# Wider step ranges for the projection blocks of a fused double attention, and its first output made in two passes

## The chip, the core and the metric

The kernel runs on one core of a Trainium2 chip. The core has a matrix engine (TensorE, PE in the profile; its weight loads are PEld), a vector engine (VectorE, DVE), a scalar engine (ScalarE, ACT), a general engine (GpSimd, POOL) and a sequencer that here issues nearly all DMAs (SyncE, SP). The metric is the device time of one execution in microseconds (us), lower is better.

## The reference

Two attentions, A and B, each with 32 heads of 20 features, read the same x; a gate mixes their results.

```python
x = A_x                                          # 1 x 2048 x 640
g = sigmoid((x * gate_w).sum(-1, keepdims=True))
def mha(x, wqkv, wo):                            # A_wqkv, A_wo or B_wqkv, B_wo
    qkv = (x @ wqkv).reshape(1, 2048, 3, 32, 20)
    q, k, v = ...                                # each 1 x 32 x 2048 x 20
    p = softmax(q @ k^T * 20 ** -0.5)
    return (p @ v).reshape(1, 2048, 640) @ wo
return g * mha(x, A_wqkv, A_wo) + (1 - g) * mha(x, B_wqkv, B_wo)
```

Inputs and output are float32.

## The kernel before

**Tiling.** The 64 heads of both attentions are taken in 16 groups of four (index g; groups 0 to 7 are A's, z = 0, groups 8 to 15 are B's, z = 1). The queries of a group are taken in four blocks of 512 (qb), and the 2048 keys in eight pairs of tiles of 128. One pair of key tiles, for one query block and four heads, is a **step** G; there are 16 x 4 x 8 = 512 steps, 32 to a group. Below, b is the first step of a group.

**What a step does.** Eight score matmuls (line 632) go into PSUM banks, and ACT turns each into weights with an exponential (`pt`, line 635). The step also applies the weights of the step before to the values: sixteen matmuls into `acc` (line 650), in two groups, V. And, some 15 steps ahead, it computes the row maxima that the softmax subtracts: eight matmuls (line 574), whose results DVE reduces (`mpart`, line 585); some go through ACT and a custom DVE operation first (lines 578, 582). When the maxima of a query block are complete, `finish_max` writes them to DRAM (`m_scr`, line 606) and back as four extra rows of the queries' tile QT (line 610), so that the score matmul itself subtracts them; the scores of that query block cannot begin before these rows are there.

**Blocks.** The projections have to be made beside the attention. They are cut into blocks of matmuls (line 375), one PSUM bank each: `project_a` makes keys and the first 48 query features of a group (4 chunks of 512 rows, three blocks of 15 matmuls each, drained by ACT into `fs`, line 402, and split by POOL into two float16 parts, `cq`); `project_r` makes the remaining query features of four groups (`rk`); `project_v` makes the values of two groups (two blocks to a pair of row tiles). `out_tiles` makes a row tile of an output: its blocks multiply stored attention results (`o_in`) with `wo`. The sum over features is cut into jobs; a job that is not the first loads the partial result `y_scr`, adds to it on DVE (line 717) and stores it again; the first one scales on ACT (line 715).

**What sets the order.** Everything is placed at build time. `fill` holds entries (first step, due step, number of blocks, generator). `slot` takes the able entry that is due first and puts out one block. Each step's order is one of three strings in `STEP`: without a block, with one (X at the start) and with two (X at both ends). Which one is decided by `behind`: two if, taking able entries by due step, their blocks do not fit one a step. `at` and `tasks` place other work (weight loads, weight maxima, splits) at given steps.

**Spreading.** Once two chunks of `project_a` are there, `later` copies them by DMA from `cq` and `rk` into the rows of QT and KT (`spread`, lines 421 and 423, all issued by SP), two halves of 18 copies each, and four copies of key differences into KD. It starts no earlier than step b+1 of the group before the one it is for, because QT and KT have two buffers and the group before that one has just finished with its own.

Of the kernel before, what the change touches and what calls it, by code (L numbers as in the profile page):

```python
# [21 lines left out]
D = 640  # L22
H = 32
DH = 20
NT = S // P
NC = D // P
GH = 4
NG = H // GH
GF = GH * DH
QB = 512  # L30
NQ = S // QB
# [3 lines left out]
VW = DH + 1  # L35
XE = 7
QKS = 2.0 ** -12
PARTS = (0, 176, 344, 512)
OB = 3
OWAIT = 20  # L40
SUM0, SUM1 = -8, 1.9


STEP = ("e0 m1 V e1 m0 e0 m1 e1 m0 e0 m1 e1 m0 V e0 m1 e1 m0",
# [17 lines left out]
def kernel(  # L62
# [148 lines left out]
    def scales_qk(i, maxima):  # L211

        return scales(maxima, 2, lambda r, inv: set_qk(i, r, inv))
# [114 lines left out]
    def weights_a(g):  # L328

        st = {}  # L330

        def load():
            i = g % NG
            t = st["t"] = wts.tile([P, NC, 160], F32, name="wstage", tag="wstage", bufs=2)
            w = wqkv[g // NG].rearrange("(c p) f -> p c f", p=P)
            nc.sync.dma_start(t[:, :, 0:GF], w[:, :, D + i * GF:D + (i + 1) * GF])
            nc.sync.dma_start(t[:, :, GF:P], w[:, :, i * GF:i * GF + 48])

        def split():
            hi, lo = blk["a", g] = block_tiles("a")  # L340
            for c0, c1, part in ((0, GF, 1), (GF, P, 0)):
                split_weights(st["t"][:, :, c0:c1], r_qk[g // 4][:, part:part + 1], hi[:, :, c0:c1], lo[:, :, c0:c1],
                              2 - 2 * part)

        return load, split
# [4 lines left out]
    def weights_r(i):  # L350

        st = {}

        def load():
            t = st["t"] = wts.tile([P, NC, 160], F32, name="wstage", tag="wstage", bufs=2)
            w = wqkv[i // 2].rearrange("(c p) f -> p c f", p=P)
            for j in range(4):
                f = (4 * (i % 2) + j) * GF + 48
                nc.sync.dma_start(t[:, :, 32 * j:32 * j + 32], w[:, :, f:f + 32])

        def split():
            hi, lo = blk["r", i] = block_tiles("r")
            rest_tiles(i)
            split_weights(st["t"][:, :, :P], r_qk[i][:, 0:1], hi, lo)

        return load, split

    def mms(i, out_ap, pairs, cost):

        if now[0] >= 0:  # L370
            tick_block(len(pairs) * cost * T_SCORE, free_at[i])
        for k, (a, b) in enumerate(pairs):
            if now[0] < 0:
                tick_block(cost * T_SCORE, free_at[i])
            nc.tensor.matmul(out_ap, a, b, start=(k == 0), stop=(k == len(pairs) - 1))  # L375
            if now[0] < 0:
                yield
# [3 lines left out]
        for _ in range(n if now[0] >= 0 else 0):  # L381
            yield

    def project_chunk(w, hi, lo, ch):

        wh, wl = w
        def pairs(n):
            if now[0] < 0:
                return ([(wh[:, c, :], b[:, c, n]) for c in range(NC) for b in (xh, xl)]
                        + [(wl[:, c, :], xh[:, c, n]) for c in range(NC)])  # L390
            return [(a[:, c, :], b[:, c, n]) for c in range(NC) for a, b in ((wh, xh), (wh, xl), (wl, xh))]

        t0 = ch * QB
        if now[0] >= 0:
            f = work.tile([P, QB], F32, name="fs")
            for k in range(3):
                if k:
                    yield
                m = slice(PARTS[k], PARTS[k + 1])
                i, pt = take()  # L400
                yield from mms(i, pt[:, m], pairs(slice(t0 + m.start, t0 + m.stop)), 0.34)
                nc.scalar.activation(f[:, m], pt[:, m], AF.Copy, scale=QKS)  # L402
                give(i, spend("act", 0.25, clock["done"]))
            nc.gpsimd.tensor_copy(hi, f)  # L404
            nc.gpsimd.tensor_tensor(lo, f, hi, op=OP.subtract)
        else:
            i, pt = take()
            yield from mms(i, pt, pairs(slice(t0, t0 + QB)), 1)
            give(i, spend("dve", T_MAX, spend("act", T_EXP, clock["done"])))
            nc.scalar.activation(hi, pt, AF.Copy, scale=QKS)  # L410
            nc.vector.scalar_tensor_tensor(lo, pt, QKS, hi, op0=OP.mult, op1=OP.subtract)
# [33 lines left out]

    def project_r(i, ch):
        n = slice(ch * QB, (ch + 1) * QB)
        yield from project_chunk(blk["r", i], rk[i][:, 0, n], rk[i][:, 1, n], ch)
        r_done.add((i, ch))

    def half_tiles(g):
# [22 lines left out]
    def project_a(g, ch):  # L474
        if ch % 2 == 0:
            half_tiles(g)
        hl = blk["q", g]
        n = slice((ch % 2) * QB, (ch % 2 + 1) * QB)
        yield from project_chunk(blk["a", g], hl[:, 0, n], hl[:, 1, n], ch)
        if ch == 1:  # L480
            key_differences(g, hl, work.tile([P, QB], F32, name="fs"), work.tile([P, 2, QB], F16, name="dd", bufs=1))
        if ch % 2 == 1:
            def later():
                for _ in range(10):
                    yield
                while not {(g // 4, c) for c in (ch - 1, ch)} <= r_done or now[0] < (g - 1) * NQ * NS + 1:
                    yield
                if ch == 1:
                    yield from spread_differences(g)
                yield from spread(g, hl, ch // 2 * 1024, 1024)  # L490
                spread_done.add((g, ch // 2))

            side.append(later())
# [478 lines left out]
    def at(G, f):  # L972
        todo.setdefault(G, []).append(f)
# [5 lines left out]
    def tasks(G, gap, fs):  # L979
        for k, f in enumerate(fs):  # L980
            at(G + k * gap, f)

    at(4, sigmoids)
    for g in range(2 * NG):
        b = g * NQ * NS
        n = g + 1
        if n < 2 * NG:
            fill += [(b - 8, b + 4 + ch, 3, project_a(n, ch)) for ch in range(4)]
            if n + 1 < 2 * NG:
                tasks(b + 15, 3, weights_a(n + 1))  # L990
            i = g // 4 + 1
            if i < 4:
                if g % 4 == 0:
                    z, c0 = i // 2, 320 * (i % 2)
                    parts = max_tasks([[(wqkv[z], part * D + c0 + 160 * k) for k in range(2)] for part in range(2)],
                                      lambda m, i=i: scales_qk(i, m))
                    tasks(b + 2, 2, parts)
                if g % 4 == 2:
                    tasks(b + 18, 3, weights_r(i))
                if g % 4 == 3:  # L1000
                    fill += [(b - 9, b + 4 + ch, 3, project_r(i, ch)) for ch in range(4)]
            gg = g // 2 + 1
            if gg < NG and g % 2 == 0:
                load, scale, split = weights_v(gg)
                at(b, load)
                at(b + 3, lambda scale=scale: side.append(scale()))
                at(b + 7, split)
                fill += [(b + 10, b + 14 + 3 * j, 2, project_v(gg, j)) for j in range(0, NT, 2)]
    for z in range(2):
        b = (6, 12)[z] * NQ * NS  # L1010
        parts = max_tasks([[(wo[z], 160 * k) for k in range(4)]], lambda m, z=z: scales_o(z, m), wrow[z])
        tasks(b + 8, 1, parts)
        b = ((NG - 1) * NQ * NS + 4, (NG + 5) * NQ * NS - 4)[z]
        for i in range(4):
            tasks(b + 3 * i, 2, out_weights(z, i))
    at((2 * NG - 1) * NQ * NS + 9, last_weights)
    at(STEPS - 4, last_picks)


    jobs = [(0, 0, NC, True, y_scr), (1, 0, 3, False, y_scr), (1, 3, NC, False, y_sum)]  # L1020
    step = NQ * NS
    outs = [(NG * step + 2 + int(9 * t), jobs[0], t) for t in range(NT)]
    outs += [((NG + 5) * step + 8 + int(3.3 * t), jobs[1], t) for t in range(NT)]
    outs += [((NG + 7) * step + SUM0 + int(SUM1 * t), jobs[2], t) for t in range(NT)]
    flow = []

    def features_stored(job, t):
# [4 lines left out]
    def out_tasks(G):  # L1032
        flow[:] = [f for f in flow if "done" not in f]
        over = (2 * NG - 1, 1) in spread_done and {(NG - 1, j) for j in range(NT)} <= v_done
        if outs and outs[0][0] <= G and len(flow) < (OB if outs[0][1][4] is y_sum else 2) and features_stored(*outs[0][1:]) and (
                over or outs[0][1][4] is not y_sum):
            G0, job, t = outs.pop(0)
            state = {"due": G0 + 10}
            flow.append(state)
            side.append(out_tiles(job, t, state))  # L1040
        if last and all(4 * last[0][0] + t in summed for t in range(4)):
            soon(now[0] + 6, 4, last_tiles(*last.pop(0)))
# [134 lines left out]
```

## Time and profile before

| | |
|---|---|
| timed runs | 2835.19 us median of 3 (2835.04 to 2835.29) |
| profiled execution, first to last instruction (span) | 2832.8 us; the profile gives no other time for it |
| granted TensorE clock, mean | 0.996 |
| busy: PE, DVE, ACT, POOL | 2773.1, 2443.8, 2529.7, 671.8 us |

Busy time is the union of an engine's instruction times. A row of the groups has line, engine, operation, tiles out and in, shapes and number; behind the bar the busy time and the mean of one in ns; behind the next bar the idle time of the engine just before them and what ended it. SP's rows are times at which it issues a DMA, not the transfer.

### The profile page before, as it was taken

How to read it: one execution, taken by the hardware profiler on the slowest of the kernel's cores; microseconds unless marked ns; L12 is line 12 of the kernel's file. 1: busy time of each engine (PE TensorE's matmuls, PEld its weight loads, DVE VectorE, ACT ScalarE, POOL GpSimd, SP SyncE). 2: the span in 40 equal slices, each digit the busy share in tenths (PEclk: the TensorE clock that was granted, in tenths of full speed). 3: DMA queues.
4: the chain of work that ended last, by engine and by line, in shares of the span. 5: the costliest groups of instructions: out<-in, count | busy, mean ns of one | idle time of the engine just before them, and what ended most of it. 6: DMA issues, size and time to landing. Idle time of an engine off the chain costs nothing.

```text
span 2832.8 us, 62443 instructions
## 1 busy us (share of the span) xinstructions
PE 2773.1 (98%) x23362; PEld 970.8 (34%) x23362; DVE 2443.8 (86%) x4763; ACT 2529.7 (89%) x5122; POOL 671.8 (24%) x914
## 2 busy tenths in 40 slices
PE   6999999999999999999999999999999999999998
PEld 3533223342323323343233333334333333332222
DVE  6688999879999898988989888887888989989982
ACT  3799999989999999989999999998899999888887
POOL 5312113231221212233431111222112233120011
PEclk9999999999999999999999999999999999999999
DMA  4110101001020101202021020211202112122222
GB/s 135 35 45 7 39 6 42 16 16 29 13 52 16 37 11 27 47 13 50 17 56 44 14 60 16 48 37 24 49 15 61 38 38 70 55 71 60 63 60 74
DMA packets 167170, 113.71 MB, mean 40 GB/s; under 512 B 102224, under 2 KB 140808, under 8 KB 166864
## 3 DMA queue, kind: packets, MB, share of 16 engines
q1 hardware_dynamic: 164320, 108.09, 15.6%
q8 instruction: 183, 3.00, 0.4%
q0 software_dynamic: 1600, 0.96, 0.2%
q14 instruction: 123, 1.01, 0.1%
q10 hardware_dynamic: 944, 0.66, 0.1%
HBM read 48.89 MB, written 26.61 MB: 27 GB/s over the span
## 4 chain that ended last, share of the span: by engine, by line
PE 91%; DVE 5%; ACT 1%; DMA 1%; POOL 1%; issue 1%; SPq 0%; POOLq 0%; DVEq 0%; ACTq 0%
PE acc L650 34%; PE bank L375 20%; PE bank L632 19%; PE bank L574 17%; DVE mpart L585 3%; ACT pt L635 1%; DVE rl L582 1%; DMA xs<-in_A_x_dram 0%; ACT rl L578 0%; DMA wv<-in_A_wqkv_dram 0%; DVE ot L736 0%; PE bank L813 0%; PE bank L183 0%; PE bank L862 0%; DVE wmax L227 0%
## 5 line engine op out<-in xcount | busy, mean ns | idle before, releaser
L635 ACT ACTIVATE pt<-bank 128x512 f32<-128x512 f32 x4096 | 2157.5, 614 | 155.0 <-PE bank L632 75.1
L585 DVE TENSOR_REDUCE mpart<-bank 128x1 f32<-128x512 f32 x2976 | 1867.8, 681 | 264.3 <-PE bank L574 167.1
L650 PE MATMUL acc<-pt,v 128*21 128x512 f32 x8192 | 1082.0, 600 | 3.4 <-DVE ot L736 3.1
L632 PE MATMUL bank<-qt,kt 64*128 64x512 f16 x4096 | 1056.3, 380 | 11.9 <-ACT pt L635 4.5
L574 PE MATMUL bank<-kt,qt 60*128 60x512 f16 x3536 | 1013.0, 380 | 4.0 <-DVE mpart L585 0.7
L574 PEld LDWEIGHTS <-qt 60*128 60x128 f16 x4096 | 235.4, 94 | 686.6 <-issue 629.0
L632 PEld LDWEIGHTS <-kt 64*128 64x128 f16 x4096 | 248.1, 94 | 456.7 <-issue 322.8
L582 DVE CUSTOM_DVE_ANT_0 rl<-bank,rl 128x512 f32<-128x512 f32 x560 | 377.5, 678 | 20.5 <-ACT rl L578 8.2
L578 ACT ACTIVATE rl<-bank 128x512 f32<-128x512 f32 x560 | 329.8, 595 | 14.6 <-PE bank L574 12.3
L744 POOL TENSOR_TENSOR ot<-ot,sq 128x512 f32<-128x512 f32 x63 | 66.0, 1047 | 993.0 <-DVE sq L741 993.0
L650 PEld LDWEIGHTS acc<-pt,v 128*21 128x21 f32 x8192 | 143.0, 99 | 434.6 <-issue 421.5
L375 PE MATMUL bank<-xx,wbh 128*128 128x168 f16 (+2 forms) x2240 | 280.1, 244 | 3.2 <-ACT xx L866 1.9
L375 PE MATMUL bank<-xx,wbl 128*128 128x168 f16 (+2 forms) x1120 | 252.8, 243 | 0.0
L375 PEld LDWEIGHTS <-wbh 128*128 128x128 f16 x2240 | 183.6, 98 | 86.8 <-issue 79.8
L574 PE MATMUL bank<-kd,qt 60*128 60x512 f16 x560 | 203.6, 381 | 1.7 <-DMA kd<-dd 1.2
L375 PE MATMUL bank<-wvh,xx 128*128 128x160 f16 (+1 forms) x1280 | 155.4, 234 | 0.5 <-ACT pt L635 0.3
L375 PE MATMUL bank<-woh,o_in 128*128 128x160 f16 (+1 forms) x960 | 155.7, 256 | 0.0
L375 PEld LDWEIGHTS <-xx 128*128 128x128 f16 x1920 | 131.6, 97 | 52.7 <-issue 49.4
L404 POOL CAST cq<-fs 128x512 f16<-128x512 f32 x60 | 36.6, 609 | 446.0 <-ACT fs L402 444.0
L375 PE MATMUL bank<-wvl,xx 128*128 128x160 f16 (+1 forms) x640 | 137.3, 231 | 0.6 <-POOL wvl L315 0.6
L375 PEld LDWEIGHTS <-o_in 128*128 128x128 f16 (+1 forms) x1440 | 104.0, 97 | 75.3 <-issue 62.2
L402 ACT ACTIVATE fs<-bank 128x168 f32<-128x168 f32 (+1 forms) x216 | 67.5, 313 | 56.6 <-PE bank L375 40.0
(131 smaller groups left out, 1305.2 us busy)
## 6 DMA issues: line engine op xcount, KB each, us to landing
y_scr<-y_out SPq DMA_DIRECT2D x32, 320.0 KB
kt<-cq SPq DMA_DIRECT2D x120, 80.0 KB
o_scr<-on SPq DMA_DIRECT2D x240, 40.0 KB
kt<-cq SPq DMA_DIRECT2D x136, 40.0 KB
xs<-in_A_x_dram SPq DMA_DIRECT2D x8, 640.0 KB
o_in<-o_scr SPq DMA_DIRECT2D x32, 160.0 KB
y_out<-y_scr SPq DMA_DIRECT2D x16, 320.0 KB
xx<-y_scr SPq DMA_DIRECT2D x16, 320.0 KB
```

Source lines behind the costliest of these rows:

```text
L375: nc.tensor.matmul(out_ap, a, b, start=(k == 0), stop=(k == len(pairs) - 1))
L402: nc.scalar.activation(f[:, m], pt[:, m], AF.Copy, scale=QKS)
L404: nc.gpsimd.tensor_copy(hi, f)
L574: nc.tensor.matmul(pt, QT[g % 2][r, pair, q0:q0 + P], k, start=True, stop=True)
L578: nc.scalar.activation(relus[u, j], pt, AF.Relu)
L582: nc.vector.tensor_tensor_reduce(rl, pt, rl, 1.0, LOW, OP.add, OP.max, m)
L585: nc.vector.tensor_reduce(m, pt, axis=AX.X, op=OP.max)
L632: nc.tensor.matmul(et, KT[g % 2][r, pair, kt * P:(kt + 1) * P], QT[g % 2][r, pair, qb * QB:(qb + 1) * QB], start=True, stop=True)
L635: nc.scalar.activation(pt, et, AF.Exp, scale=factor(g // 4))
L650: nc.tensor.matmul(acc[32 * h:32 * h + VW, :], V[(g // 2) % 2][:, kt, (g % 2) * GH + h, :], ptiles.pop((G, kk, h)), start=(kt == 0), stop= ...
L744: nc.gpsimd.tensor_tensor(t3, t3, sq.unsqueeze(2).to_broadcast([P, 16, 32]), op=OP.mult)
```

## The change

Entries of `fill` for the projections get earlier first steps and other due steps, so that their ranges are wider: `project_a` for the next group may begin 24 steps before the group that precedes it (`AFROM`) instead of 8, `project_v` has two groups' time, `project_r` moves one group ahead. Weight loads, maxima, scales and splits move with them; the scale of the last value weights is made at step 341 (`VEARLY`). The first output (A's) was one job over all five feature chunks in A's second half of time, from step 258; it becomes two jobs, chunks 0 to 2 from step 166 on and chunks 3 to 4 from step 268 on, the second of which adds to `y_scr`. Since `width` is 320 for up to three chunks, its blocks go from 160 to 320 columns. `FINE` is empty, so all blocks of `project_a` and `project_r` keep their three cuts.

```diff
-PARTS = (0, 176, 344, 512)
+THIRDS = (0, 176, 344, 512)
+QUARTERS = (0, 128, 256, 384, 512)
+FINE = ()
 OB = 3
 OWAIT = 20
-SUM0, SUM1 = -8, 1.9
+AFROM, ADUE, ADUES = -24, -8, 4
+QKMAX = (0, 10, 42, 10)
+VEARLY = 338
+OMAX, OSPLIT = (134, 346), (151, 362)
+OUTS = ((166, 5.2), (257, 5.8), (398, 4.5), (466, 2.5))
+OWAITS = (40, 20, 20, 10)
...
+    step = NQ * NS
     for g in range(2 * NG):
-        b = g * NQ * NS
+        b = g * step
         n = g + 1
         if n < 2 * NG:
-            fill += [(b - 8, b + 4 + ch, 3, project_a(n, ch)) for ch in range(4)]
+            parts = 4 if n in FINE else 3
+            fill += [((-8, 15)[g] if g < 2 else b + AFROM, b + ADUE + ADUES * ch if g else 4 + 3 * ch, parts, project_a(n, ch))
+                     for ch in range(4)]
             if n + 1 < 2 * NG:
-                tasks(b + 15, 3, weights_a(n + 1))
+                tasks(b + 2 if g else 9, 3, weights_a(n + 1))
...
-                    tasks(b + 2, 2, parts)
+                    tasks(b + QKMAX[i], 2, srcs)
                 if g % 4 == 2:
-                    tasks(b + 18, 3, weights_r(i))
-                if g % 4 == 3:
-                    fill += [(b - 9, b + 4 + ch, 3, project_r(i, ch)) for ch in range(4)]
+                    tasks(b + 6, 3, weights_r(i))
+                    parts = 4 if 4 * i in FINE else 3
+                    fill += [(b + 12, b + 22 + 4 * ch, parts, project_r(i, ch)) for ch in range(4)]
             gg = g // 2 + 1
             if gg < NG and g % 2 == 0:
                 load, scale, split = weights_v(gg)
-                at(b, load)
-                at(b + 3, lambda scale=scale: side.append(scale()))
-                at(b + 7, split)
-                fill += [(b + 10, b + 14 + 3 * j, 2, project_v(gg, j)) for j in range(0, NT, 2)]
+                at(max(b - 8, 0), load)
+                if gg < NG - 1:
+                    at(max(b - 5, 3), lambda scale=scale: side.append(scale()))
+                at(max(b - 1, 7), split)
+                fill += [(max(b + 2, 10), b + 2 * step - 4 + j // 2, 2, project_v(gg, j)) for j in range(0, NT, 2)]
...
-    jobs = [(0, 0, NC, True, y_scr), (1, 0, 3, False, y_scr), (1, 3, NC, False, y_sum)]
-    step = NQ * NS
-    outs = [(NG * step + 2 + int(9 * t), jobs[0], t) for t in range(NT)]
...
+    jobs = [(0, 0, 3, True, y_scr), (0, 3, NC, False, y_scr), (1, 0, 3, False, y_scr), (1, 3, NC, False, y_sum)]
+    outs = [(b + int(every * t), job, t) for job, (b, every) in zip(jobs, OUTS) for t in range(NT)]
```

The changed kernel has nine lines more, so line 635 of before is 642 after, and so on by 7 in that part (421 is 428, 606 is 613).

Three places in the order of instructions show what moves. On ScalarE at step 89, late in group 2, before (`fs` drains a projection block, `rl` is a maximum that goes through ScalarE, `pt` are the exponentials, of which a step has eight):

```order
L402 ACTIVATE fs<-bank_91 128x168
L402 ACTIVATE fs<-bank_93 128x168
L578 ACTIVATE rl<-bank_94 128x512
L635 ACTIVATE pt<-bank_95 128x512
L635 ACTIVATE pt<-bank_91 128x512
L635 ACTIVATE pt<-bank_90 128x512
L635 ACTIVATE pt<-bank_93 128x512
```

The same place now, with the end of step 88 ahead of it:

```order
L642 ACTIVATE pt<-bank_90 128x512
L642 ACTIVATE pt<-bank_92 128x512
L642 ACTIVATE pt<-bank_89 128x512
L409 ACTIVATE fs<-bank_93 128x168
L642 ACTIVATE pt<-bank_95 128x512
L585 ACTIVATE rl<-bank_92 128x512
L642 ACTIVATE pt<-bank_94 128x512
```

Two drained blocks in the step have become one. On ScalarE at the border of steps 39 and 40, in the middle of group 1, before and then now:

```order
L635 ACTIVATE pt<-bank_91 128x512
L635 ACTIVATE pt<-bank_95 128x512
L635 ACTIVATE pt<-bank_94 128x512
L578 ACTIVATE rl<-bank_92 128x512
L635 ACTIVATE pt<-bank_90 128x512
L635 ACTIVATE pt<-bank_93 128x512
L635 ACTIVATE pt<-bank_89 128x512
```

```order
L642 ACTIVATE pt<-bank_91 128x512
L642 ACTIVATE pt<-bank_93 128x512
L642 ACTIVATE pt<-bank_89 128x512
L409 ACTIVATE fs<-bank_90 128x176
L642 ACTIVATE pt<-bank_92 128x512
L585 ACTIVATE rl<-bank_94 128x512
```

A step that had no block has one. On SP at the start of group 1, where the copies for group 2 are issued, before: `m_scr` is the write of a query block's maxima, `qt<-m_scr` their return, the other rows are copies of `spread`:

```order
L606 DMA m_scr_124<-m4r 16x4x32 x4
L421 DMA qt_80<-cq 40x1x1024
L423 DMA qt_80<-cq 20x1024
L421 DMA qt_80<-rk 40x1x1024
L423 DMA qt_80<-rk 20x1024
L610 DMA qt_81<-m_scr_124 4x512 x4
L421 DMA kt_82<-cq 40x1x1024
L423 DMA kt_82<-cq 20x1024
```

The same place now:

```order
L613 DMA m_scr_124<-m4r 16x4x32 x4
L428 DMA qt_80<-cq 40x1x1024
L430 DMA qt_80<-cq 20x1024
L428 DMA qt_80<-rk 40x1x1024
L430 DMA qt_80<-rk 20x1024
L617 DMA qt_81<-m_scr_124 4x512 x4
L763 DMA o_scr_121<-on 20x2x512 x4
```

Before, 18 copies stood ahead of the write of the maxima, four between it and their return, and 18 behind. Now 36 stand ahead of the write, four between, and none behind: attention results (`o_scr`) follow at once.

More of the change, by code (lines that the diff above doesn't have):

```diff
@@ L382, in turns, with project_chunk @@
             yield
-    def project_chunk(w, hi, lo, ch):
+    def project_chunk(w, hi, lo, ch, parts=THIRDS):
         wh, wl = w
@@ L395, in project_chunk @@
             f = work.tile([P, QB], F32, name="fs")
-            for k in range(3):
+            for k in range(len(parts) - 1):
                 if k:
                     yield
-                m = slice(PARTS[k], PARTS[k + 1])
+                m = slice(parts[k], parts[k + 1])
                 i, pt = take()
-                yield from mms(i, pt[:, m], pairs(slice(t0 + m.start, t0 + m.stop)), 0.34)
+                yield from mms(i, pt[:, m], pairs(slice(t0 + m.start, t0 + m.stop)), (m.stop - m.start) / QB)
                 nc.scalar.activation(f[:, m], pt[:, m], AF.Copy, scale=QKS)
@@ L447, in project_r @@
         n = slice(ch * QB, (ch + 1) * QB)
-        yield from project_chunk(blk["r", i], rk[i][:, 0, n], rk[i][:, 1, n], ch)
+        yield from project_chunk(blk["r", i], rk[i][:, 0, n], rk[i][:, 1, n], ch, QUARTERS if 4 * i in FINE else THIRDS)
         r_done.add((i, ch))
@@ L478, in project_a @@
         n = slice((ch % 2) * QB, (ch % 2 + 1) * QB)
-        yield from project_chunk(blk["a", g], hl[:, 0, n], hl[:, 1, n], ch)
+        yield from project_chunk(blk["a", g], hl[:, 0, n], hl[:, 1, n], ch, QUARTERS if g in FINE else THIRDS)
         if ch == 1:
@@ L994 @@
                     z, c0 = i // 2, 320 * (i % 2)
-                    parts = max_tasks([[(wqkv[z], part * D + c0 + 160 * k) for k in range(2)] for part in range(2)],
-                                      lambda m, i=i: scales_qk(i, m))
-                    tasks(b + 2, 2, parts)
+                    srcs = max_tasks([[(wqkv[z], part * D + c0 + 160 * k) for k in range(2)] for part in range(2)],
+                                     lambda m, i=i: scales_qk(i, m))
+                    tasks(b + QKMAX[i], 2, srcs)
                 if g % 4 == 2:
-                    tasks(b + 18, 3, weights_r(i))
-                if g % 4 == 3:
-                    fill += [(b - 9, b + 4 + ch, 3, project_r(i, ch)) for ch in range(4)]
+                    tasks(b + 6, 3, weights_r(i))
+                    parts = 4 if 4 * i in FINE else 3
+                    fill += [(b + 12, b + 22 + 4 * ch, parts, project_r(i, ch)) for ch in range(4)]
             gg = g // 2 + 1
@@ L1004 @@
                 load, scale, split = weights_v(gg)
-                at(b, load)
-                at(b + 3, lambda scale=scale: side.append(scale()))
-                at(b + 7, split)
-                fill += [(b + 10, b + 14 + 3 * j, 2, project_v(gg, j)) for j in range(0, NT, 2)]
+                at(max(b - 8, 0), load)
[3 more added lines that the diff above has]
+                fill += [(max(b + 2, 10), b + 2 * step - 4 + j // 2, 2, project_v(gg, j)) for j in range(0, NT, 2)]
+    early = weights_v(NG - 1)
+    at(VEARLY, early[0])
+    at(VEARLY + 3, lambda: side.append(early[1]()))
     for z in range(2):
-        b = (6, 12)[z] * NQ * NS
         parts = max_tasks([[(wo[z], 160 * k) for k in range(4)]], lambda m, z=z: scales_o(z, m), wrow[z])
-        tasks(b + 8, 1, parts)
-        b = ((NG - 1) * NQ * NS + 4, (NG + 5) * NQ * NS - 4)[z]
+        tasks(OMAX[z], 1, parts)
         for i in range(4):
-            tasks(b + 3 * i, 2, out_weights(z, i))
-    at((2 * NG - 1) * NQ * NS + 9, last_weights)
+            tasks(OSPLIT[z] + 3 * i, 2, out_weights(z, i))
+    at((2 * NG - 1) * step + 9, last_weights)
     at(STEPS - 4, last_picks)
-    jobs = [(0, 0, NC, True, y_scr), (1, 0, 3, False, y_scr), (1, 3, NC, False, y_sum)]
-    step = NQ * NS
-    outs = [(NG * step + 2 + int(9 * t), jobs[0], t) for t in range(NT)]
-    outs += [((NG + 5) * step + 8 + int(3.3 * t), jobs[1], t) for t in range(NT)]
-    outs += [((NG + 7) * step + SUM0 + int(SUM1 * t), jobs[2], t) for t in range(NT)]
+    jobs = [(0, 0, 3, True, y_scr), (0, 3, NC, False, y_scr), (1, 0, 3, False, y_scr), (1, 3, NC, False, y_sum)]
+    outs = [(b + int(every * t), job, t) for job, (b, every) in zip(jobs, OUTS) for t in range(NT)]
     flow = []
@@ L1037, in out_tasks @@
             G0, job, t = outs.pop(0)
-            state = {"due": G0 + 10}
+            state = {"due": G0 + OWAITS[jobs.index(job)]}
             flow.append(state)
```

## The prediction

> **What bounds the kernel now.** I read the page first, for the span and the busy shares.
>
> ```profile
> span 2832.8 us, 62443 instructions
> PE 2773.1 (98%) x23362; PEld 970.8 (34%) x23362; DVE 2443.8 (86%) x4763; ACT 2529.7 (89%) x5122; POOL 671.8 (24%) x914
> ```
>
> Three engines are close to full, so one share says little. The main loop has 512 steps, and they come in three kinds: with no projection block, with one, with two. So I next read busy time by stretches, each a run of steps of one kind (the first two excepted, which are the start). The columns are start and end, length, then for each engine busy time and number of instructions, the granted clock, DMA share and GB/s. A step without a block has 32 matmuls on PE (8 scores, 8 maxima, 16 values), and a block adds 15, or 9 or 6 in the wide output blocks; so the count beside PE tells how many steps a stretch holds (instructions cut by its edge are counted, hence a few too many).
>
> ```profile
> 96.70:174.40 77.70, 72.04 (x553) 28.66 (x553) 64.24 (x149) 62.40 (x129) 19.08 (x22) 0.98 0.21 50
> 174.40:192.40 18.00, 17.67 (x151) 6.29 (x150) 15.38 (x36) 16.52 (x36) 2.60 (x5) 1.00 0.24 53
> 357.90:395.50 37.60, 36.59 (x260) 8.56 (x261) 36.34 (x71) 36.05 (x74) 8.31 (x13) 1.00 0.03 7
> 404.80:446.80 42.00, 42.00 (x380) 15.06 (x376) 36.86 (x70) 39.12 (x80) 12.38 (x16) 1.00 0.09 20
> 508.10:549.70 41.60, 41.60 (x380) 14.69 (x382) 36.59 (x70) 39.34 (x81) 8.31 (x13) 1.00 0.12 22
> 1915.20:2003.40 88.20, 88.20 (x874) 41.35 (x876) 66.22 (x122) 73.14 (x155) 23.09 (x31) 1.00 0.14 33
> 2551.50:2572.80 21.30, 21.30 (x164) 6.74 (x164) 19.29 (x38) 18.18 (x37) 0.00 (x0) 1.00 0.19 55
> 2667.10:2697.00 29.90, 29.90 (x229) 8.79 (x228) 29.46 (x56) 27.53 (x55) 1.76 (x2) 1.00 0.19 49
> ```
>
> Row 3 is eight steps without a block (260/32): 37.60/8 = 4.70 us a step. DVE is busy 36.34 of 37.60 and ACT 36.05: they set the pace there. Rows 4 and 5 are eight steps with one block each: 5.25 (q and k rows, 168 or 176 wide) and 5.20 us (values, 160 wide), together 5.23. DVE has 36.86 of 42.00, so it has gained 5 us of idle time: PE sets the pace now. Row 6 is fourteen steps with two blocks: 88.20/14 = 6.30 us, DVE 75% and ACT 83%. The price of a block is thus 0.53 us as the first of its step and 1.07 as the second. Rows 7 and 8 are single wide output blocks of nine matmuls (four steps, 5.33 us) and of six (six steps, 4.98 us).
>
> PE's busy time cannot show this: row 3 has 36.59 of 37.60, yet 15 more matmuls a step cost half of what they cost in row 6. The Trainium skill says the same of the measure (Perfetto Trace Analysis, "Identifying the Most-Contended Engine": matmul busy time is no good sign of the nearness to the limit, since matmuls are pipelined). Taken at its word, PE's 97% in row 3 would make a moved block save nothing; rows 3 to 6 say, as the rule does, that moving one saves time.
>
> **The change: where blocks go.** Blocks counted on the engines' built order, by step (no / one / two blocks):
>
> | steps | before | after |
> |---|---|---|
> | 0 to 10 | 3 / 3 / 5 | 0 / 11 / 0 |
> | 11 to 496 | 103 / 332 / 51 | 53 / 429 / 4 |
> | 497 to 512 | 0 / 8 / 8 | 0 / 9 / 7 |
>
> Middle, at the prices above. Before: 103 x 4.70 + 332 x 5.23 + 51 x 6.30 = 2541.8 us. After: 53 x 4.70 + 429 x 5.23 + 4 x 6.30 = 2518.0. That is -23.8 us, with three more blocks (taken over from the start). Ends come from DVE's weight maxima, which the change moves:
>
> ```profile
> L227 DVE TENSOR_REDUCE wmax<-wstage 128x1 f32<-128x480 f32 x20 | 12.8, 638 | 0.0
> L227 DVE TENSOR_REDUCE wmax<-wstage 128x1 f32<-128x320 f32 x20 | 9.5, 476 | 0.0
> ```
>
> In a DVE-bound step they cost their whole time, in a PE-bound one little. A quarter of these 22.3 us moved the one way or the other is 6: -30 or -18.
>
> First output, whole before (64 blocks of 15 matmuls, 160 wide, 5.20 us a step) and now in two passes (32 blocks of nine, 32 of six, 320 wide): 32 x (5.33 - 5.20) + 32 x (4.98 - 5.20) = +4.2 - 7.0 = -2.8 us. I take -1: in row 8 DVE is busy 29.46 of 29.90, so the short blocks already stand at its limit, and the second pass adds on DVE where ACT scaled before:
>
> ```profile
> L715 ACT ACTIVATE y_out<-bank,f_o 128x160 f32<-128x160 f32 x64 | 25.2, 393 | 7.5 <-PE bank L375 6.1
> L717 DVE SCALAR_TENSOR_TENSOR y_out<-bank,f_o,y_out 128x320 f32<-128x320 f32 x32 | 17.5, 548 | 8.0 <-PE bank L375 4.7 <-issue 2.5 <-ACT pt L635 0.6
> ```
>
> So 25.2 us leave ACT, 32 x 0.548 = 17.5 us come to DVE, spread over steps where DVE idles 0.6 us each. Sixteen more loads and stores of y_scr go to SP, beside other work. Middle in all: -25 us.
>
> Start. Row 1 is steps 0 to 10 (77.7 us, 13 blocks in ten and a half steps); row 2 is the next three, one block each, while the maxima still run ahead at one and a half times the rate: 6.0 us a step. Ten and a half steps at 6.0 make 63, that is -15 us at best. At worst only the two blocks that leave count, 2 x 1.07 = -2. Between them I take -8: rest waits of the first value weights' scale, and DVE's 64.24 us of row 1, of which only two weight maxima leave, stay.
>
> Tail, one block fewer among the last sixteen steps: -1 us, of
>
> ```profile
> 2749.10:2832.80 83.70, 74.70 (x533) 23.81 (x531) 24.33 (x51) 62.59 (x127) 10.07 (x16) 0.95 0.21 70
> ```
>
> The weight loads, scales and splits only change their steps; their DVE and POOL work is the same, and the round trip of a scale through PE and DVE still falls into a PE-bound or a DVE-bound step as often as before. Nothing.
>
> Sum: -25 - 8 - 1 = -34 us. The profiled execution's span of 2832.8 becomes 2798.8; the timed runs' median lies 2.4 above the span (2835.2), so **2801.2 us**.
>
> **What is moved on SP.** Projection of the next group now ends before its group of steps begins, so all 40 copies that spread it into QT, KT and KD are free to go at once. The order shows what falls behind them: the running maxima of query block 1 (L606 and L610 before, L613 and L617 now), which the scores of step b+8 read, b being the group's first step. Before, 22 copies went ahead of L610 and 18 after; now all 40 go ahead, and two weight loads. Prices from one such place, SP's issues:
>
> ```profile
> 461.71 1.72 SPq L606 DMA_DIRECT2D m_scr<-m4r  x4
> 463.48 0.83 SPq L421 DMA_DIRECT2D qt<-cq  x1
> 464.35 0.73 SPq L423 DMA_DIRECT2D qt<-cq  x1
> 465.12 0.79 SPq L421 DMA_DIRECT2D qt<-rk  x1
> 465.96 0.72 SPq L423 DMA_DIRECT2D qt<-rk  x1
> 466.85 1.36 SPq L610 DMA_DIRECT2D qt<-m_scr  x4
> 351.92 0.40 SPq L336 DMA_DIRECT2D wstage<-in_A_wqkv_dram  x1
> 352.37 0.52 SPq L337 DMA_DIRECT2D wstage<-in_A_wqkv_dram  x1
> SPq L610 <- DMA m_scr<-m4r: 46.3, 52, 2.6
> ```
>
> A pair of copies takes 1.64 us (463.48 to 465.12), 0.82 each. The second half's copies overwrite keys that the scores of step b-1 read, so most start at b: 39 x 0.82 + 0.92 + 1.72 + 1.36 = 36.0, and 46.3/52 = 0.9 for the wait between the last two, 36.9 us. Step b+8 comes after 8 x 5.23 = 41.8 us: 4.9 left, less one landing, which nothing here prices but that wait, so about 4. Where the eight steps have no block (37.6 us, the group at step 160) nothing is left; with the copies of two output tiles, some 3 us, about 1. I take no stall, and put 0 to 10 us for a few groups into the range. The Trainium skill would put a DMA's fixed part at about 2 us (DMA: Bandwidth & Descriptors, "Anatomy of one DMA", measured on GpSimd's path). By it the landing would take 1 us more, and the margin would be 3.
>
> **The rivals.**
> *Late maxima (slower).* SP becomes the bound at each group's start: PE waits at step b+8, and behind its score matmul wait the maxima, values and blocks of its queue, so DVE and ACT run dry. For it: the margin fell from 18 copies' worth (15 us more) to 4. Against it: the sum above. It decides from about 4 us of added delay; to lose the 34 us, fourteen groups would have to wait 2.4 us each, that is, rows landing 6 to 7 us later than I figure. With 8 us: 14 x 4 = 56, so 2857 us. Chance 0.08.
>
> *No price difference (same).* If PE were as full in row 3 as its busy time says, every block would cost 1.07 us wherever it lies. The middle would gain 47 x 1.07 and pay 50 x 1.07, +3 us, and start and tail would keep -9: -6, so 2829 us. Against it stand rows 3 to 6 directly. Chance 0.06.
>
> *The change does not level the blocks.* The table above is the built order, so this is excluded.
>
> **How the numbers follow.** The forecast, levelling paid at the measured prices, has 0.86. What this kernel's measurement can tell from no change is about 0.2%, 5.7 us. Range: -49 (-30 in the middle, -15 start, -4 for first output and tail) gives 2786; -15 (-18 middle, -5 start, -1 tail, and 9 us of late rows) gives 2820. Rivals lie outside it, 0.14 together. Faster by over 0.2%: 0.86. Same: the second rival and weak forms of the first, 0.06. Slower: 0.08.
>
> **What would show it.** Right: in the profile after, steps of the stretches with one block still at 5.2 to 5.25, no long run at 6.3, DVE's idle time spread evenly, LDWEIGHTS count lower (first output in 30 instead of 60 matmuls a tile), steps 0 to 10 within about 70 us. Wrong: score matmuls (L639) waiting for the maxima's rows, longest at the eighth step of each group; one-block steps at 5.4 or more because DVE or ACT stays behind; a gain of the middle under 15 us although two-block steps are gone.

## The result, and the profile after

The changed kernel takes 2809.15 us (median of 4 runs, 2807.89 to 2809.72) against 2835.11 us: ratio 0.991, 95% interval 0.9899 to 0.9922. It is 26 us faster; 34 were forecast. The page of the kernel after, span and busy time:

```profile
span 2807.9 us, 61401 instructions
## 1 busy us (share of the span) xinstructions
PE 2752.2 (98%) x22882; PEld 936.9 (33%) x22882; DVE 2452.8 (87%) x4795; ACT 2526.1 (90%) x5090; POOL 671.6 (24%) x914
```

480 matmuls are gone, as 16 tiles of the first output now take 30 instead of 60. DVE has gained 9 us of work, ACT has lost 4.

Busy time by stretches of the kernel after (start and end, length, busy time and instructions of PE, PEld, DVE, ACT and POOL, granted clock, DMA share, GB/s): the start (steps 0 to 10), the three steps after it, eight steps without a block, eight with a key and query block each, eight with a block of `project_r` (one of these eight has an output block of nine matmuls instead):

```profile
96.70:168.70 72.00, 68.70 (x518) 24.70 (x516) 61.65 (x143) 61.32 (x125) 17.23 (x20) 0.95 0.14 33
168.70:186.80 18.10, 17.79 (x150) 6.31 (x149) 15.76 (x36) 16.67 (x36) 8.95 (x13) 1.00 0.13 26
411.60:451.20 39.60, 38.12 (x262) 9.01 (x261) 38.53 (x82) 36.27 (x73) 8.50 (x10) 1.00 0.06 14
534.60:576.50 41.90, 41.90 (x378) 15.10 (x376) 36.55 (x70) 39.23 (x81) 7.23 (x11) 1.00 0.03 6
1242.70:1284.70 42.00, 42.00 (x372) 14.78 (x370) 36.56 (x70) 39.23 (x81) 8.97 (x13) 1.00 0.06 13
```

A step with one block costs what it cost before: 41.90/8 = 5.24 and 42.00/8 = 5.25 us. Row 3 has 39.60/8 = 4.95 because a value weights' scale falls into it: DVE has 82 instructions there, not 71, and is busy 38.53 of 39.60. The tail of the kernel after, from step 497 on, in the same view:

```profile
2726.80:2807.90 81.10, 72.70 (x527) 22.53 (x525) 23.76 (x50) 62.41 (x127) 10.08 (x16) 0.97 0.20 70
```

So the span's 24.9 us divide into 77.7 - 72.0 = 5.7 in the start, 83.7 - 81.1 = 2.6 in the tail, and 16.6 in the middle, for which 25 were forecast. Step by step, the middle holds one step of 13.4 us where its neighbours take 5 (from the second set of value matmuls of one step to that of the next, 1657.08 to 1670.45 below). PE's waits in the kernel after name it (engine, tile and line, releaser; total us, times, longest):

```profile
PE bank L382 <- DMA o_in<-o_scr: 6.1, 1, 6.1
```

The timeline around it, PE and SP of the kernel after:

```profile
1657.08 1.06 PE L657 MATMUL acc<-pt,v 128*21 128x512 f32 x8
...
1661.65 0.80 SPq L428 DMA_DIRECT2D qt<-rk  x1
1662.56 0.93 SPq L699 DMA_DIRECT2D o_in<-o_scr  x2
1663.54 0.47 SPq L704 DMA_DIRECT2D y_out<-y_scr  x1
1664.05 0.75 SPq L430 DMA_DIRECT2D qt<-rk  x1
...
1664.75 0.45 PE L382 MATMUL bank<-woh,o_in 128*128 128x320 f16 x1 [6.07 <-DMA o_in<-o_scr]
...
1670.45 1.06 PE L657 MATMUL acc<-pt,v 128*21 128x512 f32 x8
```

An output block in step 295 (group 9, seven steps in) multiplies `o_in`, whose loads (L699) SP issued at 1662.56, behind almost all of the spread's copies. PE stood 6.07 us for them. Everything behind that block in PE's queue stood too, so DVE and ACT idled 7.3 us each.

### The profile page after: what moved, and what is told of

It reads as the page before. It is cut to its first block, busy times and chain, and to the rows that moved or that the text cites. A ratio compares the mean times of both kernels' runs of the same rounds, so it can differ in the third digit from the quotient of the medians.

```text
span 2807.9 us, 61401 instructions
## 1 busy us (share of the span) xinstructions
PE 2752.2 (98%) x22882; PEld 936.9 (33%) x22882; DVE 2452.8 (87%) x4795; ACT 2526.1 (90%) x5090; POOL 671.6 (24%) x914
## 3 DMA queue, kind: packets, MB, share of 16 engines
q1 hardware_dynamic: 170096, 118.99, 16.9%
## 4 chain that ended last, share of the span: by engine, by line
PE 90%; DVE 4%; ACT 2%; DMA 1%; SPq 1%; POOL 1%; issue 1%; POOLq 0%; ACTq 0%; DVEq 0%
PE acc L657 34%; PE bank L382 19%; PE bank L581 19%; PE bank L639 18%; DVE mpart L592 3%; ACT pt L642 1%; DVE rl L589 1%; DMA xs<-in_A_x_dram 0%; ACT rl L585 0%; SPq L428 0%; PE bank L820 0%; SPq L430 0%; DMA wv<-in_A_wqkv_dram 0%; PE bank L190 0%; DVE ot L743 0%
## 5 line engine op out<-in xcount | busy, mean ns | idle before, releaser
L581 PE MATMUL bank<-kt,qt 60*128 60x512 f16 x3536 | 1025.2, 381 | 4.5 <-ACT pt L642 1.2
L639 PEld LDWEIGHTS <-kt 64*128 64x128 f16 x4096 | 238.0, 94 | 274.6 <-issue 155.1
L382 PE MATMUL bank<-woh,o_in 128*128 128x320 f16 (+1 forms) x640 | 156.4, 302 | 6.2 <-DMA o_in<-o_scr 6.1
L757 POOL CAST on<-ob 128x512 f16<-128x512 f32 x63 | 38.4, 609 | 329.3 <-DVE ob L754 285.4
L382 PEld LDWEIGHTS <-o_in 128*128 128x128 f16 (+1 forms) x960 | 80.9, 97 | 98.4 <-issue 64.2
```

The source lines that it names most:

```text
L581: nc.tensor.matmul(pt, QT[g % 2][r, pair, q0:q0 + P], k, start=True, stop=True)
L639: nc.tensor.matmul(et, KT[g % 2][r, pair, kt * P:(kt + 1) * P], QT[g % 2][r, pair, qb * QB:(qb + 1) * QB], start=True, stop=True)
L757: nc.gpsimd.tensor_copy(o[:, 0], ot)
```

## The experiments

**Pacing the copies.** The second half's copies wait until the first half's are issued: 8 a step instead of 16. No block moves.

```diff
-                while not {(g // 4, c) for c in (ch - 1, ch)} <= r_done or now[0] < (g - 1) * NQ * NS + 1:
+                while not {(g // 4, c) for c in (ch - 1, ch)} <= r_done or now[0] < (g - 1) * NQ * NS + 1 or (
+                        ch == 3 and (g, 0) not in spread_done):
```

> The changed kernel, but the copies of a group's second half wait until the first half's are issued, so that SP has 8 of them a step instead of 16; blocks stay where the change put them. Theory: the one wait of 8.2 us in step 295 (an output tile's loads behind the copies on SP) is what the measured gain lacks against the step prices. Then this kernel is 8 us faster than the changed one: span 2799 to 2801 us, median 2800 to 2802, and no step of the middle over 7 us. Rival: the wait comes from the tile's transfer itself or from the wider blocks; then the median stays at 2808 to 2810.

Measured: 2801.92 us (2801.66 to 2802.00), ratio 0.9883 (0.9867 to 0.990); in a second session 2801.99. SP's timeline of this kernel at the same tile:

```profile
1647.31 0.79 SPq L428 DMA_DIRECT2D qt<-rk  x1
1648.20 0.94 SPq L700 DMA_DIRECT2D o_in<-o_scr  x2
1649.18 0.47 SPq L705 DMA_DIRECT2D y_out<-y_scr  x1
```

The loads leave at 1648.20 instead of 1662.56, PE's wait for `o_in` is not in the table any more, and no step of the middle exceeds 7 us. The shortfall of 8 us was this one wait. Paced, the kernel is 33 us below before and beats both kernels; in the other expectations it is called e1_paced.

**The other end of the same wait.** The copies stay bunched; the second pass's tiles wait 40 turns instead of 20 between loads and blocks.

```diff
-        for _ in range(OWAIT):
+        for _ in range(40 if job is jobs[1] else OWAIT):
```

> The changed kernel, in which the second pass of the first output waits 40 instead of 20 turns (five steps instead of two and a half) between issuing a tile's loads and its blocks; the copies stay bunched. Counts 55 / 425 / 6, so +1 to +2 us by the prices. Theory (a tile's loads stood behind the copies on SP): the wait of 8.2 us goes, 2801 to 2804 us. Rival: the copies delay other things too (the maxima's rows or keys), then it stays above 2806.

Measured: 2802.84 us (2802.80 to 2802.92), ratio 0.9889 (0.9873 to 0.9904). So bunching itself costs nothing that can be seen: one tile's loads were late behind the copies, the maxima's rows were not.

**More copies.** The changed kernel with 16 more issues at each group's start.

```diff
...
+                    for k in range(16):
+                        nc.sync.dma_start(dump[k], hl[:20, 0])
+                        yield
...
```

> The changed kernel with 16 more copies (20 rows of 2 KB to an unused place in DRAM) on SP at the start of each group from 1 on, among the copies of the spread. At about 0.77 us each they delay the return of the maxima by 12 us. In the changed kernel the last issue of that return stands 7.2, 7.2, 8.2, 7.2, 5.4, 3.7, 6.7, 10.6, 6.6, 15.5, 22.5, 23, 8.3, 5.6 and 22 us ahead of the step that needs it (groups 1 to 15), and about 1.2 us go for the landing. Theory (late rows cost what they are late): eleven groups lose 12 + 1.2 less their margin, some 65 to 75 us, so 2875 to 2885 us; by the margin of 4 us that was predicted it would be over 100. Rival (the return is hidden in another way, or SP catches up): under 2820 us.

Measured: 2881.34 us (2879.59 to 2882.15), ratio 1.0162 (1.0145 to 1.0179). The total is the one expected, its parts are not. PE's waits of this kernel:

```profile
PE bank L383 <- DMA o_in<-o_scr: 37.4, 4, 14.9
PE bank L649 <- DMA qt<-m_scr: 21.3, 8, 5.3
```

And SP's timeline in it, where the extra copies are `dump`:

```profile
319.42 0.73 SPq L431 DMA_DIRECT2D qt<-cq  x1
320.19 0.50 SPq L507 DMA_DIRECT2D dump<-cq  x1
320.74 0.82 SPq L429 DMA_DIRECT2D kt<-cq  x1
```

An extra copy took 0.50 us, not 0.77, so they added some 9 us at each start, not 12. Late maxima's rows cost eight waits, 21.3 us in all; output tiles behind the copies cost 37.4 in four. The rival of the prediction is a real mechanism, and 16 more copies suffice to turn the gain into a loss; but of the two waits the loads of `o_in`, which the prediction had not thought of as victims, are the larger (6.1 of their 37.4 us the changed kernel has too). What else makes up the 72 us over the changed kernel is not taken apart here; a part is the slower clock after such waits (last section). That the sum came out as expected is chance.

**Two blocks, then none.** The paced kernel with the same blocks put two into each even step of 32 to 447 and none into the odd ones; and in a second kernel two a step for eight steps, none for the next eight.

In the second kernel the condition is `G % 16 < 8`. The lines that both have beside the pacing:

```diff
...
+        if 32 <= G < 448 and blocks == 1:
+            blocks = 2 if G % 2 == 0 else 0
```

> As e1_paced, but in steps 32 to 447 the same blocks are put two into each even step and none into each odd one (239 steps without a block, 57 with one, 190 with two among steps 11 to 496, for 53, 429, 4). Theory A, the price belongs to each single step: 239 x 4.70 + 57 x 5.23 + 190 x 6.30 = 2618 us for the middle instead of 2518, so +100 us over e1_paced: about 2900. Theory B, the price belongs to a run (DVE and ACT catch up within two steps, since their work reaches seven banks ahead): a pair costs 2 x 5.23, so within 10 us of e1_paced.

> As e1_paced, but in steps 32 to 447 blocks go two a step for eight steps and then none for eight (236 steps without a block, 63 with one, 187 with two among steps 11 to 496). Both theories of the pairs agree here: 236 x 4.70 + 63 x 5.23 + 187 x 6.30 = 2617 us for the middle, +99 us over e1_paced, 2895 to 2905 us.

Measured: pairs 2921.64 us (ratio 1.0306, 1.0288 to 1.0323), runs of eight 2916.84 us (1.0288, 1.0271 to 1.0305). Eight steps of the pairs, in the view by stretches:

```profile
500.90:545.40 44.50, 44.33 (x376) 15.66 (x376) 37.37 (x69) 39.19 (x81) 18.06 (x21) 1.00 0.03 6
```

These are the 376 matmuls of eight steps with one block each (41.90 us after, x378), with the same ACT work, in 44.50 us: 11.13 us a pair, where 4.70 + 6.30 = 11.00 was reckoned, and 2 x 5.24 = 10.48 for two single ones. That agrees with theory A in time, but it does not decide between the theories, since on PE the pairs are no lumps. The order string of a step with two blocks has one at either end, so between two blocks of the pairs lies the work of one step, 32 matmuls, just as with one block a step. Two stretches of the same trace, each from the first matmul of a block to the first of the next:

```profile
502.56:508.53 5.97, 5.88 (x50) 2.05 (x48) 5.46 (x13) 5.18 (x12) 5.04 (x4) 1.00 0.01 3
508.53:513.75 5.22, 5.22 (x50) 1.87 (x48) 4.39 (x9) 4.68 (x11) 2.62 (x6) 1.00 0.01 2
```

The first holds a step in the order without a block, the second one in the order with two; so it goes on, about 5.9 and 5.2 us in turn. What the pairs change is thus the order of scores, maxima and values within the steps, and the loss shows in the steps of the first order (a single-block step took 5.2). The step prices belong to kinds of steps as the program writes them, blocks and order together. How far DVE and ACT catch up across a step's border, the pairs do not show; a kernel with another order string at the same places of the blocks was not run. The runs of eight are true lumps: there PE has two blocks directly behind each other, and then none for about eight steps.

The whole came to 120 and 115 us over the paced kernel instead of 100. With 186 and 183 more two-block steps, moving a block from a two-block step to an empty one is worth 120/186 = 0.64 and 115/183 = 0.63 us rather than 0.54: the price was 15 to 20% low.

**The parts alone.** Only the ranges of blocks, the outputs as before:

```diff
-OMAX, OSPLIT = (134, 346), (151, 362)
-OUTS = ((166, 5.2), (257, 5.8), (398, 4.5), (466, 2.5))
-OWAITS = (40, 20, 20, 10)
+OMAX, OSPLIT = (200, 392), (228, 412)
+OUTS = ((258, 9), (424, 3.3), (472, 1.9))
+OWAITS = (10, 10, 10)
...
-    jobs = [(0, 0, 3, True, y_scr), (0, 3, NC, False, y_scr), (1, 0, 3, False, y_scr), (1, 3, NC, False, y_sum)]
+    jobs = [(0, 0, NC, True, y_scr), (1, 0, 3, False, y_scr), (1, 3, NC, False, y_sum)]
```

> The changed kernel with the outputs as before (first output in one pass of 160-wide blocks from step 258, with the old steps for its weights). Counts of steps 11 to 496: 73 without a block, 390 with one, 23 with two. By the step prices the middle is 73 x 4.70 + 390 x 5.23 + 23 x 6.30 = 2527.7 us, 14.1 less than before; with the start (5.7, as the changed kernel's trace shows) and a tail like before's: -20 us, 2815 us. If one-block steps were dearer than their price for want of DVE or ACT time, it would be over 2822.

Measured: 2815.49 us, ratio 0.9934 (0.992 to 0.9948), 19 us. Only the first output in two passes, on the kernel before:

```diff
...
-    jobs = [(0, 0, NC, True, y_scr), (1, 0, 3, False, y_scr), (1, 3, NC, False, y_sum)]
+    jobs = [(0, 0, 3, True, y_scr), (0, 3, NC, False, y_scr), (1, 0, 3, False, y_scr), (1, 3, NC, False, y_sum)]
...
-    outs = [(NG * step + 2 + int(9 * t), jobs[0], t) for t in range(NT)]
...
+    outs = [(180 + int(5.2 * t), jobs[0], t) for t in range(NT)]
+    outs += [(268 + int(5.8 * t), jobs[1], t) for t in range(NT)]
...
```

> The kernel before with the first output alone changed: two passes of 320-wide blocks, from steps 180 and 268 on, its weights made from step 150 on. Counts of steps 11 to 496: 96 / 346 / 44. By the prices 2538.0 us for the middle, -3.8, and -1 to -3 for the wider blocks: 2829 to 2832 us. Rival: the second pass on DVE and its loads cost more than the blocks save: 2836 us or more.

Measured: 2831.13 us, ratio 0.9989 (0.998 to 0.9998), 3.4 us. The two alone make 22, and together, without the wait, 33: the first output in the first half fills more of the empty steps when the wider ranges let the other blocks make room (53 empty and 4 double steps together, 73 and 23 or 96 and 44 alone). By the prices these counts give 6 of the 11 us; the rest is not taken apart.

Only the start, on the kernel before:

```diff
-            fill += [(b - 8, b + 4 + ch, 3, project_a(n, ch)) for ch in range(4)]
+            fill += [(b - 8, b + 4 + (ch if g else 3 * ch), 3, project_a(n, ch)) for ch in range(4)]
```

> The kernel before with only group 1's projection blocks spread over the first twelve steps (due steps 4, 7, 10, 13 instead of 4, 5, 6, 7): steps 0 to 10 go from 3 / 3 / 5 to 0 / 11 / 0. Prediction's theory: -8 for the start; what the changed kernel's trace shows is 5.7 us over steps 0 to 10. Two blocks fall into steps 11 and 12 or later here, where they cost about 0.53 each. So 2829 to 2831 us. Rival (the start is bound by DVE and ACT, and the blocks are not what makes its steps long): 2834 or more.

Measured: 2831.72 us, ratio 0.999 (0.9981 to 0.9999), 2.8 us, a little under what was expected. The start of this kernel by the view of stretches:

```profile
96.70:169.80 73.10, 68.92 (x523) 24.71 (x523) 63.29 (x147) 62.09 (x126) 17.25 (x20) 0.98 0.16 39
```

77.7 us have become 73.1, and the later steps give back some of it, with two blocks more. The change's 72.0 has weight maxima moved out as well (DVE 61.65 for 63.29).

**The tail.** The paced kernel with the second output's passes at other steps, seven blocks earlier.

```diff
-OUTS = ((166, 5.2), (257, 5.8), (398, 4.5), (466, 2.5))
+OUTS = ((166, 5.2), (257, 5.8), (402, 4.0), (462, 2.1))
```

> As e1_paced, with the second output's two passes from steps 402 (every 4.0) and 462 (every 2.1) instead of 398 (4.5) and 466 (2.5): seven blocks go from the last sixteen steps, which then have 2 / 12 / 2 instead of 0 / 9 / 7, into steps 448 to 496, and steps 11 to 496 have 47 / 434 / 5. By the step prices the middle pays 4.3 us more (6 x 4.70 less, 5 x 5.23 and 1 x 6.30 more); in the last steps, where the changed kernel's trace has 3.97 us with one block or two at the low end and 4.89 at the high end, seven blocks at 0.92 us less make -6.4. Theory: about 2 us faster than e1_paced, 2799 to 2801. Rival (the last steps are bound by ACT or by the last tiles): the same as e1_paced or up to 4 us slower.

> e1_paced once more, beside e9_tail on the same chip, as the kernel that it is compared with: 2802 us.

Measured: 2801.59 us (2800.45 to 2802.70) beside 2801.99 (2801.46 to 2804.28) for the paced kernel. The medians differ by 0.4 us and the runs overlap: whether anything was gained can't be told.

## Why the prediction was right, and where it was off

- **Step prices: right for this change.** One-block steps stayed at 5.24. Without the wait the middle gained 16.6 + 8.4 = 25.0 us (13.4 us for that step, against 5.0), the forecast's 25. The pairs and the runs of eight put a moved block at 0.63 to 0.64 us instead of 0.54, which for some 50 blocks would be 5 us more than was found; what took these is not settled, so that the middle came out to the microsecond is partly luck. What the prices rest on, "DVE and ACT set the pace" without a block and PE with one, fits the busy times; but a kind of step differs in its order too, and the pairs show that the order counts.
- **"I take no stall, and put 0 to 10 us for a few groups into the range": the term that was off.** It measured 8.4 us, at one place. The mechanism, SP's queue behind forty copies, was the one named, and the victim was another: I followed the maxima's rows and read the output tiles' copies only as 3 us of delay for these, not as loads with a due time of their own, two and a half steps after their place in the program. For the maxima's rows 4.9 us of room, before the landing, were predicted. The kernel after has 3.7 us in the tightest group (6), 7 in groups 1, 2 and 4 and up to 23 later; no score matmul waits for these rows. The timeline of the kernel after in group 2, SP's two issues and the first score matmul that reads the rows:

```profile
476.27 1.82 SPq L613 DMA_DIRECT2D m_scr<-m4r  x4
481.51 1.35 SPq L617 DMA_DIRECT2D qt<-m_scr  x4
...
490.02 0.39 PE L639 MATMUL bank<-qt,kt 64*128 64x512 f16 x1
```

- **Start, -8: 5.7, and 4.6 without the moved weight maxima.** The term that was off is the price of 6.0 us from the three steps after the start. These had 36 DVE instructions, 12 a step; the start has 143 in ten and a half, 13.6, since the maxima run ahead for all of it. DVE and ACT are busy 61.7 and 61.3 of 72.0 us; that this extra work holds the start is argued from these counts, and no run isolates it. The clock has a small part: it is 0.95 in this row, for 0.98 before. With the same start, the ranges-alone kernel has 0.98 there and takes 1 us less (75.0 for 76.0 us, from the first score matmul of step 0 to that of step 11).
- **First output, -1: within a few us.** Alone it gained 3.4 where counts of steps gave 3.8, so nothing can be seen that the wider blocks brought of their own. One reading in this part was wrong, without weight in the sum: 25.2 us do not leave ACT, since the first pass still scales there, in 32 wider blocks; 25.2 - 16.9 = 8.3 us left it. The row of the kernel after:

```profile
L722 ACT ACTIVATE y_out<-bank,f_o 128x320 f32<-128x320 f32 x32 | 16.9, 528 | 6.2 <-PE bank L382 4.7
```

- **Tail, -1: 2.6.** Not split further; the experiment on the tail could not tell.
- **Late maxima (slower):** real, shown with 16 more copies; not reached by the change, which has 3.7 us or more between issue and use. **No price difference (same):** excluded, by the result (26 us, for 6) and by the 115 us for runs of eight.

The 2809.15 us lie inside the range of 2786 to 2820. Sum as measured: -5.7 - 2.6 - 25.0 + 8.4 = -24.9 us of span, -33 without the wait, for -34.

## What to carry to other kernels

Where several engines are each nearly full, price a unit of work by the length of whole steps with none, one and two units of it, not by busy shares: the first unit in a step cost 0.53 us here, the second 1.1, and levelling paid that difference. Such a price is one of the whole step, with the order in which its work is written: the pairs kept the distance between the blocks on PE, changed the order of the other work, and lost 120 us. When work is made ready earlier, look at what it releases: transfers that used to trickle become a burst on one issuing queue, and every load that stands behind the burst in program order, not only the one you watch, needs its own margin. A single such wait took a quarter of the gain.

## What the runs showed of the hardware that was not expected

A wait of PE costs more than its length. The step of the wait, in the view by stretches of the kernel after:

```profile
1657.10:1670.40 13.30, 7.23 (x40) 1.51 (x38) 5.11 (x10) 4.54 (x10) 0.00 (x0) 0.74 0.39 101
```

The granted clock, 1.00 in the stretches around it, averages 0.74 here. Cut finer, into PE's last work before the wait, most of the wait, the end of it with the work behind it, and what follows:

```profile
1652.10:1658.70 6.60, 6.57 (x52) 1.76 (x50) 6.20 (x14) 6.27 (x13) 1.54 (x3) 1.00 0.42 116
1658.70:1662.80 4.10, 0.00 (x0) 0.00 (x0) 1.08 (x2) 1.12 (x3) 0.00 (x0) 1.00 0.20 38
1662.90:1669.60 6.70, 4.85 (x20) 1.07 (x20) 2.34 (x4) 1.57 (x3) 0.00 (x0) 0.50 0.58 161
1669.70:1676.40 6.70, 6.70 (x58) 1.86 (x54) 5.83 (x11) 5.92 (x12) 0.00 (x0) 1.00 0.28 71
```

The clock fell to half some 4 us after PE had stopped, and came back some 5 us after it had started again. PE's timeline has the same matmul in the block before the wait and in the one after it:

```profile
1654.21 0.30 PE L382 MATMUL bank<-wol,o_in 128*128 128x320 f16 x1
...
1664.99 0.47 PE L382 MATMUL bank<-wol,o_in 128*128 128x320 f16 x1
```

It took 0.47 us for 0.30. So 6.07 us of waiting lengthened the step by 8.4 us. The Trainium skill (TensorE: Matmul & The Clock Gate, "The HAM clock gate") has the clock halved after an idle window of about 3.4 us and restored after as much activity. The trace agrees in kind, with about 4 and 5 us, and the added 2.3 us is the price of it here. With 16 more copies the mean clock of the whole run fell to 0.986 from 0.995.
